# A routing count made by one matrix product, or by two without a clearing, in an attention–MoE–FFN kernel

## The chip, the cores and the metric

The kernel runs on one core of one Trainium2 chip. Its time is the device time of one launch in microseconds; the kernel before was run three times, with a median of 765.33 us (763.8 to 768.46). One further execution was taken by the hardware profiler; every row below is from that one. The core's engines are PE (TensorE, the matrix engine; PEld is its weight load), DVE (VectorE), ACT (ScalarE), POOL (GpSimd) and SP (SyncE, which here only issues transfers). Each engine works through its own list of instructions in order.

## The reference, cut to what matters

Three stages follow each other, all in float32. Four batches of 576 tokens, eight heads of 64, go through an attention with 128 random features; the 2304 tokens of 512 that result go through a mixture of experts (the best of 8 experts by a gate, weighted by its probability); and the result goes through a feed-forward layer of width 2048.

```python
def phi(x):
    h = np.einsum('bhsd,md->bhsm', x, omega) - np.sum(x * x, axis=-1, keepdims=True) / 2.0
    return np.exp(h - np.max(h, axis=-1, keepdims=True)) / np.sqrt(m)
kv = np.einsum('bhsm,bhsd->bhmd', k_p, v)
num = np.einsum('bhsm,bhmd->bhsd', q_p, kv)          # attn = num / (q_p . sum(k_p) + 1e-6)
logits = x @ w_gate                                   # x: attn, (2304, 512); w_gate: (512, 8)
expert_idx = np.argmax(logits, axis=1)
for e in range(E):
    mask = expert_idx == e
    out[mask] = gate_w[mask, None] * (np.maximum(x[mask] @ w1[e], 0.0) @ w2[e])
h = out @ w_in
return (h * (1.0 / (1.0 + np.exp(-1.702 * h)))) @ w_out
```

## The kernel before, in words

**Tiling.** A batch has 576 tokens: four tiles of 128 and a last one with 64 used rows (`T` is 4, `TAIL` is 64). Heads are taken in quads of four, so there are eight quads, `i` = 0 to 7, two to a batch. For each quad, keys and queries are loaded by SP (`m`, L253 and L258), split into two float16 halves (`hl`, ACT L307 and POOL L308), transposed by a transfer from chip memory to chip memory that SP issues (`DMA_TRANSPOSE xT<-hl`, L309), and multiplied with omega on PE (`pr`, L350 and L351). DVE takes maxima (L359, L368) and subtracts (`qp`, `kp`, L380), ACT takes the exponential (L376, L386). Queries are turned on PE (`tq`, L430, with ACT `qpT`, L432) and multiplied with `kv` (`num`, L444); the result is turned back (`tx`, L464; its last 64 rows go to `small`, L466) into the token matrix `xh`/`xl`, two halves whose sum is the float32 value.

**Routing.** When both quads of batch b are done, `route_steps` runs for it: the logits (`lT`, `lg_ps`, `lg`), the row maximum `rm` (L549), the one-hot `oh` (L551, 128 rows by 5 tiles by 8 experts; in tile 4 the rows from 64 on hold no token), the clearing of these rows (L552), the exponentials `ex`, and the count per expert: a product of a matrix of ones with `oh` (`ct_ps`, L561), summed over the tiles (`ct`, L565). The largest count (`cm`, `ci`) gives the batch's main expert `es` (L571). SP reads `es` into a register (L604) and loads that expert's weights, each transfer one `st` (L674). ACT and POOL (for some, DVE) split each into halves `wh` (L698) and `wl` (L700).

**Experts and the rest.** The expert's products on PE (`m_ps`, L136, three products to one of float32) run between the attention steps of the next batches, with `h1h` on ACT (L732) and `h1l` on DVE (L735). The tokens that chose another expert than the batch's main one are counted (`total`); a general path at the end, which is not entered with these inputs, would treat them. From about 400 us on PE does the feed-forward layer (`qa`, L1146 and L1249).

**What sets the order.** The program is written as generators that take turns. Then a scheduler goes over the whole program: it simulates the engines with its own costs, and each engine's list comes out in the order that this simulation gives. One operation that becomes shorter or is gone changes the simulated times, and with them the lists of all engines. Accumulator banks are shared by name: `lT_ps`, `lg_ps`, `ct_ps` and some of the `num` use the one bank "n", so what is written there next waits for the reading of what was there before. In the lists below, [waits ...] names the counters that an instruction waits for; DMAHW0 to DMAHW7 are dealt in turn to the transfers, and the issue of a transfer waits until the earlier one with the same counter has landed.

Of the kernel before, what the change touches and what calls it, by code (L numbers as in the profile page):

```python
# [22 lines left out]
def kernel(  # L23
# [13 lines left out]
    nc = tc.nc  # L37
# [6 lines left out]
    T = 4  # L44
    TAIL = S - T * P
# [97 lines left out]
    ones = const.tile([P, P], F32, name="ones")  # L143
# [367 lines left out]
    def route(b):  # L511
        g = route_steps(b)
        while True:
            with tc.high_priority() if b < HP_ROUTE else nullcontext():
                c = next(g, "end")
            if c == "end":
                return
            yield c

    def route_steps(b):  # L520
# [14 lines left out]
        for t in range(T + 1):  # L535
# [13 lines left out]
        nc.vector.tensor_reduce(out=rm, in_=lg, axis=AX.X, op=ALU.max)  # L549
        oh = att.tile([P, T + 1, E], F32, tag="oh", name="oh", bufs=2)  # L550
        nc.vector.tensor_tensor(out=oh, in0=lg, in1=rm.to_broadcast([P, T + 1, E]), op=ALU.is_equal)  # L551
        nc.vector.memset(oh[TAIL:, T, :], 0.0)  # L552
        ex = att.tile([P, T + 1, E], F32, tag="ex", name="ex", bufs=2)
        nc.vector.tensor_tensor(
            out=ex, in0=lg, in1=rm.to_broadcast([P, T + 1, E]), op=ALU.subtract
# [3 lines left out]
        yield 0  # L559
        ct_ps = pp.tile([P, T + 1, E], F32, tag="n", name="ct_ps", bufs=1)  # L560
        nc.tensor.matmul(  # L561
            out=ct_ps.rearrange("p t e -> p (t e)"), lhsT=ones, rhs=oh.rearrange("p t e -> p (t e)")
        )
        ct = att.tile([P, E], F32, tag="ct", name="ct", bufs=2)
        nc.vector.tensor_reduce(out=ct, in_=ct_ps.rearrange("p t e -> p e t"), axis=AX.X, op=ALU.add)  # L565
        cm = att.tile([P, 8], F32, tag="cm", name="cm", bufs=2)
# [9 lines left out]
        if b == B - 1:  # L576
            dg = att.tile([P, T * P + TAIL], F32, tag="dg", name="dg", bufs=1)
            for t in range(T + 1):
                n = P if t < T else TAIL
                nc.scalar.activation(  # L580
                    out=dg[:n, t * P:t * P + n], in_=ident[:n, :n], func=ACTF.Copy, scale=gate[:n, t, :]
# [5 lines left out]
        for t in range(T + 1):  # L587
# [9 lines left out]
            out=rr[:, :, 0:1], in0=eq, scalar=-float(2 * E), in1=ixf, op0=ALU.mult, op1=ALU.add  # L597
# [12 lines left out]
            out=r_dram[b * S:b * S + T * P].rearrange("(p t) c -> p t c", t=T), in_=rr[:, 0:T]  # L610
# [380 lines left out]
    def general_w(pool, f, s):  # L991
        raw = load_raw(pool, s, f)
        w = pool.tile([P, DM], I32, tag="dec", name="dec", bufs=2)
        decode(w, raw)
        hi = pool.tile([P, DM], F32R, tag=f"w{s}h", name=f"w{s}h", bufs=2)
        lo = pool.tile([P, DM], F32R, tag=f"w{s}l", name=f"w{s}l", bufs=2)
        split(hi, lo, f32(w))
        return hi, lo

    if True:  # L1000
# [399 lines left out]
        p = hp.tile([P, SETW], F32R, tag="y2", name="p2", bufs=1)  # L1400
# [29 lines left out]
    with tc.If(more > 0), tc.tile_pool(name="gp", bufs=1) as gp:  # L1430
        with tc.For_i(0, NT // P, 1) as w:
# [21 lines left out]
            with tc.For_i(0, E, 1) as e:  # L1453
# [6 lines left out]
                with tc.If(cnt > 0):  # L1460
# [3 lines left out]
                    for f in range(NF1):  # L1464
                        wa = gp.tile([P, KD, P], F32, name="wa", bufs=2)
                        nc.sync.dma_start(
                            out=wa,
# [5 lines left out]
                        for kk in range(KD):  # L1473
                            nc.tensor.matmul(
                                out=ps, lhsT=wa[:, kk], rhs=xT[:, kk], start=(kk == 0), stop=(kk == KD - 1)
# [4 lines left out]
                    for dt in range(KD):  # L1480
                        wb = gp.tile([P, NF1, P], F32, name="wb", bufs=2)
                        nc.sync.dma_start(
                            out=wb,
# [5 lines left out]
                        for f in range(NF1):  # L1489
                            nc.tensor.matmul(  # L1490
                                out=ps, lhsT=wb[:, f], rhs=ha[:, f], start=(f == 0), stop=(f == NF1 - 1)
# [6 lines left out]
                    for f in range(NF2):  # L1498
                        wh, wl = general_w(gp, f, 0)
                        oh, ol = general_w(gp, f, 1)  # L1500
# [44 lines left out]
```

## Time and profile before

| what | value |
|---|---|
| median of three runs | 765.33 us (763.8 to 768.46) |
| profiled execution, its time | 766.79 us |
| its span, first to last instruction | 764.9 us |
| instructions | 14360 |
| PE busy | 737.1 us, 96% of the span |
| PEld, DVE busy | 715.1 us (93%), 527.5 us (69%) |
| ACT, POOL busy | 337.5 us (44%), 131.8 us (17%) |

A busy share tells how much of the span an engine had an instruction under way. PE's 27.8 us without one are in a few places; the granted clock (PEclk, in parts of full speed, where 1.00 is 2.4 GHz and 0.50 is 1.2 GHz) tells where a busy PE worked at half its speed. A transfer has two times: how long SP was held by issuing it (the row's own time), and how long it took from the start of the issue to its landing.

### The profile page before, as it was taken

To read this page: it belongs to the slowest core of one execution; us is meant where nothing else is said; L and a number is where in the kernel's file an instruction comes from. 1 tells how busy PE (TensorE), PEld (TensorE's weight loads), DVE (VectorE), ACT (ScalarE), POOL (GpSimd) and SP (SyncE) were. 2 spreads that over 40 slices of the span, in tenths; PEclk is the share of its full clock that TensorE was granted. 3 is DMA by queue.
4 is the path that set the end of the run, shared out by engine and by line. 5 is a ranking of instruction groups with operands and counts; after the bars stand their busy time and mean duration, and the time that the engine had idled before them with its cause. 6 is when DMAs were issued, how large, how long until landed. Compare 5 with 4: busy or idle time off the path is not lost.

```text
span 764.9 us, 14360 instructions
## 1 busy us (share of the span) xinstructions
PE 737.1 (96%) x5559; PEld 715.1 (93%) x5559; DVE 527.5 (69%) x1188; ACT 337.5 (44%) x638; POOL 131.8 (17%) x78
## 2 busy tenths in 40 slices
PE   7998799998999999999999999999999999999997
PEld 6877789998999999998999999999999999999996
DVE  5866848583958577655879559981368777777774
ACT  5554554334623423332427565454576443444331
POOL 3563467604900522000000000000000000000000
PEclk9999799999999999999999999999999999999999
DMA  5447495539723544558155548972978544443311
GB/s 156 116 134 187 160 234 110 136 83 250 189 71 98 169 164 141 175 172 274 59 165 197 178 167 299 320 259 101 330 276 297 171 138 138 138 126 121 114 30 31
DMA packets 136715, 127.57 MB, mean 167 GB/s; under 512 B 58176, under 2 KB 120896, under 8 KB 135744
## 3 DMA queue, kind: packets, MB, share of 16 engines
q1 hardware_dynamic: 123936, 98.85, 44.6%
q10 hardware_dynamic: 12704, 27.73, 10.5%
q8 instruction: 45, 0.74, 0.4%
q14 instruction: 30, 0.25, 0.1%
HBM read 79.68 MB, written 40.40 MB: 157 GB/s over the span
## 4 chain that ended last, share of the span: by engine, by line
PE 80%; DMA 7%; DVE 5%; POOL 3%; ACT 2%; issue 2%; SPq 1%; ACTq 0%; POOLq 0%; DVEq 0%
PE m_ps L136 17%; PE qa L1249 13%; PE qa L1146 13%; PE qm L1249 7%; PE w_ps L136 5%; DMA st<-in_moe_w_dram 4%; PE pb L1249 3%; PE qm L1146 3%; PE qu L1146 3%; PE num L444 2%; POOL wl L700 2%; PE kv_ps L402 2%; PE qn L1146 2%; PE qt L1146 2%; DMA m<-in_k_dram 1%
## 5 line engine op out<-in xcount | busy, mean ns | idle before, releaser
L1146 PE MATMUL qa<-y,wi 128*128 128x384 f32 x576 | 109.2, 337 | 0.4 <-DVE g L901 0.4
L1146 PEld LDWEIGHTS qa<-y,wi 128*128 128x128 f32 x576 | 101.4, 188 | 0.8 <-DVE g L901 0.8
L136 PE MATMUL m_ps<-xh,wh 128*128 128x288 f32 x256 | 77.8, 304 | 0.7 <-DVE h1l L735 0.7
L136 PE MATMUL m_ps<-xh,wl 128*128 128x288 f32 x256 | 76.0, 298 | 0.0
L136 PE MATMUL m_ps<-xl,wh 128*128 128x288 f32 x256 | 75.8, 296 | 0.0
L700 POOL TENSOR_TENSOR wl<-st,wh 128x1024 fp32r<-128x1024 f32 x23 | 55.1, 2403 | 108.2 <-ACT wh L698 108.2
L359 DVE TENSOR_REDUCE small<-pr 128x4 f32<-128x512 f32 (+1 forms) x80 | 51.0, 638 | 16.1 <-PE pr L351 12.3
L698 ACT ACTIVATE wh<-st 128x1024 fp32r<-128x1024 f32 (+1 forms) x33 | 34.0, 1033 | 44.0 <-DMA st<-in_moe_w_dram 32.7
L735 DVE SCALAR_TENSOR_TENSOR h1l<-m_ps,h1h 128x288 fp32r<-128x288 f32 x64 | 28.9, 454 | 34.0 <-ACT h1h L732 34.0
L732 ACT ACTIVATE h1h<-m_ps 128x288 fp32r<-128x288 f32 x64 | 25.8, 405 | 55.3 <-PE m_ps L136 53.9
L136 PEld LDWEIGHTS m_ps<-xh,wh 128*128 128x128 f32 x256 | 48.1, 188 | 1.7 <-DVE h1l L735 1.4
L136 PE MATMUL m_ps<-h1h,wh 128*128 128x288 f32 x160 | 49.2, 307 | 0.0
L136 PEld LDWEIGHTS m_ps<-xl,wh 128*128 128x128 f32 x256 | 48.1, 188 | 0.1
L136 PEld LDWEIGHTS m_ps<-xh,wl 128*128 128x128 f32 x256 | 48.0, 188 | 0.2
L136 PE MATMUL m_ps<-h1h,wl 128*128 128x288 f32 x160 | 47.7, 298 | 0.3 <-POOL wl L700 0.3
L136 PE MATMUL m_ps<-h1l,wh 128*128 128x288 f32 x160 | 47.6, 297 | 0.0
L1249 PE MATMUL qa<-p,p 128*128 128x256 f32 x360 | 46.1, 282 | 1.1 <-DVE p L855 0.8
L1249 PE MATMUL qa<-p,gs 128*128 128x256 f32 x360 | 45.9, 282 | 0.0
L1249 PEld LDWEIGHTS qa<-p,p 128*128 128x128 f32 x360 | 44.1, 189 | 1.6 <-DVE p L855 1.0
L1249 PEld LDWEIGHTS qa<-p,gs 128*128 128x128 f32 x360 | 44.2, 189 | 0.0
L432 ACT ACTIVATE qpT<-tq 128x512 f32<-128x512 f32 (+1 forms) x40 | 22.1, 552 | 43.3 <-PE tq L430 38.6
L444 PE MATMUL num<-kv,qpT 128*128 128x65 f32 (+1 forms) x320 | 39.4, 267 | 0.7 <-ACT qpT L432 0.6
(213 smaller groups left out, 1835.1 us busy)
## 6 DMA issues: line engine op xcount, KB each, us to landing
g_dram<-g ACTq DMA_DIRECT2D x48, 384.0 KB, 3.9
st<-in_moe_w_dram SPq DMA_DIRECT2D x31, 512.0 KB, 5.0
pg<-g_dram SPq DMA_DIRECT2D x10, 1024.0 KB, 5.5
raw<-in_moe_w_in_dram SPq DMA_DIRECT2D x16, 512.0 KB, 3.8
gt<-g_dram SPq DMA_DIRECT2D x8, 1024.0 KB, 5.4
p<-wo_dram SPq DMA_DIRECT2D x6, 1024.0 KB, 7.3
yt<-y_dram SPq DMA_DIRECT2D x12, 384.0 KB, 5.4
vm<-in_v_dram SPq DMA_DIRECT2D x32, 128.0 KB, 3.2
```

The lines of the kernel that those rows point to most:

```text
L136: ins = nc.tensor.matmul(out=ps, lhsT=a, rhs=b, start=start and n == 0, stop=stop and n == 2)
L359: nc.vector.tensor_reduce(out=pm, in_=ps[:, :w], axis=AX.X, op=ALU.max, negate=on_act)
L402: nc.tensor.matmul(out=kv_ps[:, h, :], lhsT=kp[j // 2][:, j % 2, h2, :], rhs=vm[:, h, t, :], start=(t == 0), stop=False,)
L432: nc.scalar.activation(out=qt[i][:, :w], in_=tq[:, :w], func=ACTF.Exp)
L444: nc.tensor.matmul(out=ps[:n, c, h2, :], lhsT=lhsT, rhs=kv[:, h, :])
L698: nc.scalar.activation(out=hi[:, :, s], in_=st[:, :, s], func=ACTF.Copy)
L700: eng.tensor_tensor(out=lo[:, :, s], in0=st[:, :, s], in1=f32(hi)[:, :, s], op=ALU.subtract)
L732: nc.scalar.activation(out=hh[:, f], in_=ps, func=ACTF.Relu)
L735: nc.vector.scalar_tensor_tensor(out=hl[:, f], in0=ps, scalar=0.0, in1=f32(hh[:, f]), op0=ALU.max, op1=ALU.subtract)
L1146: ins = nc.tensor.matmul(out=ps, lhsT=w[:, a, ks], rhs=y[:, b, kk], start=start and kk + m == 0, stop=kk == 1 and m == 2, skip_group_check ...
L1249: ins = nc.tensor.matmul(out=ps, lhsT=x[:, f], rhs=w[i][:, f], start=start and f + m == 0, stop=f == NP - 1 and m == 2, skip_group_check=True,
```

## The change

The clearing L552 goes. The product L561, which took all 128 rows of all five tiles (128x40), becomes one over the four full tiles (128x32) and one over the last tile that takes only its 64 used rows (128x8). Both write the same bank, and what follows reads it as before.

```diff
         nc.vector.tensor_tensor(out=oh, in0=lg, in1=rm.to_broadcast([P, T + 1, E]), op=ALU.is_equal)
-        nc.vector.memset(oh[TAIL:, T, :], 0.0)
         ex = att.tile([P, T + 1, E], F32, tag="ex", name="ex", bufs=2)
...
         ct_ps = pp.tile([P, T + 1, E], F32, tag="n", name="ct_ps", bufs=1)
         nc.tensor.matmul(
-            out=ct_ps.rearrange("p t e -> p (t e)"), lhsT=ones, rhs=oh.rearrange("p t e -> p (t e)")
+            out=ct_ps[:, 0:T].rearrange("p t e -> p (t e)"), lhsT=ones, rhs=oh[:, 0:T].rearrange("p t e -> p (t e)")
         )
+        nc.tensor.matmul(out=ct_ps[:, T], lhsT=ones[:TAIL, :], rhs=oh[:TAIL, T])
         ct = att.tile([P, E], F32, tag="ct", name="ct", bufs=2)
```

The lists of all engines change with it, from the first batch's routing to that of the last (PE up to about 340 us by the trace's times); behind that PE's list is the same. Three places follow.

**DVE, behind the first batch's one-hot.** `ct` is the sum over the tiles, `es` the expert's number that SP waits for; `qp`, `small` and `mx` belong to the attention, `gate`, `ixf`, `eq` and `rr` to the rest of the routing. Before:

```order
L565 TENSOR_REDUCE ct<-ct_ps 128x8
L573 TENSOR_REDUCE gate<-ex 128x5
L368 TENSOR_TENSOR small<-small,sq 128x2
L568 MAX cm<-ct 128x8
L574 TENSOR_SCALAR gate<-gate 128x5
L368 TENSOR_TENSOR mx<-small,sq 128x2
L569 MAX_INDEX ci<-cm,ct 128x8
L575 RECIPROCAL gate<-gate 128x5
L380 TENSOR_TENSOR qp<-pr,mx 128x256
L359 TENSOR_REDUCE small<-pr 128x4
L571 CAST es<-ci 128x1
```

Now:

```order
L565 TENSOR_REDUCE ct<-ct_ps 128x8
L591 CAST ixf<-lix 128x5
L380 TENSOR_TENSOR qp<-pr,mx 128x512
L359 TENSOR_REDUCE small<-pr 128x2
L568 MAX cm<-ct 128x8
L573 TENSOR_REDUCE gate<-ex 128x5
L368 TENSOR_TENSOR small<-small,sq 128x2
L569 MAX_INDEX ci<-cm,ct 128x8
L574 TENSOR_SCALAR gate<-gate 128x5
L368 TENSOR_TENSOR mx<-small,sq 128x2
L571 CAST es<-ci 128x1
```

`ct` now stands ahead of `ixf`, the 128x512 `qp` and a `small` that preceded it before; the 128x256 `qp`, the reciprocal and the 128x4 `small`, which stood ahead of `es`, now stand behind it.

**SP, behind the first eight weight transfers of the first batch.** `r_dram` are routing results, the ISA rows belong to the weight transfer's address, and the transpose brings the halves of one later quad. Before:

```order
L674 DMA st<-in_moe_w_dram 128x2x512 [waits DMAHW0_49]
L609 DMA r_dram<-rr 128x8 [waits DMAHW1_49,DVE_49]
L674 ISA
L674 DMA st<-in_moe_w_dram 128x2x512 [waits DMAHW2_49,DVE_49]
L612 DMA r_dram<-rr 64x2 [waits DMAHW3_49]
L309 DMA_TRANSPOSE xT<-hl 128x18x128 [waits DMAHW4_49,PE_49,Pool_49]
L504 DMA x_dram<-xn 64x256 [waits DMAHW6_49,DVE_49]
```

Now:

```order
L674 DMA st<-in_moe_w_dram 128x2x512 [waits DMAHW0_49]
L609 DMA r_dram<-rr 128x8 [waits DMAHW1_49,DVE_49]
L612 DMA r_dram<-rr 64x2 [waits DMAHW2_49]
L309 DMA_TRANSPOSE xT<-hl 128x18x128 [waits DMAHW3_49,PE_49,Pool_49]
L674 ISA
L674 DMA st<-in_moe_w_dram 128x2x512 [waits DMAHW5_49,DVE_49]
L504 DMA x_dram<-xn 64x256 [waits DMAHW6_49,DVE_49]
```

The transpose now goes ahead of the ninth weight transfer, and waits for the counter that the third of them holds, where it waited for the fourth's.

**PE, where the transposed tile is first read.** `LDWEIGHTS xT [waits DMAHW...]` is the first reading of what the transpose of the SP rows brings. Before, behind a `small` at 99.68 us came 24 products `m_ps` with `wh_1049` (three stand here), and then:

```order
L466 MATMUL small<-ident,xn 128x64 [waits DVE_49]
L136 MATMUL m_ps<-xh,wh_1049 128x288 [waits DVE_49]
L136 MATMUL m_ps<-xl,wh_1049 128x288
L136 MATMUL m_ps<-xh,wl_1050 128x288 [waits Pool_49]
...
L466 MATMUL small<-ident,xn 128x64 [waits DVE_49]
L444 MATMUL num<-kv,qpT 128x65 [waits DVE_49,PE_49]
L444 MATMUL num<-kv,qpT 128x65 x3
L464 MATMUL tx<-ident,xn 128x128 x2
L350 LDWEIGHTS xT [waits DMAHW4_49]
L350 MATMUL pr<-wh_117,xT 128x128 [waits Activation_49]
```

Now:

```order
L466 MATMUL small<-ident,xn 128x64 [waits DVE_49]
L350 LDWEIGHTS xT [waits DMAHW3_49]
L350 MATMUL pr<-wh_117,xT 128x128 [waits Activation_49]
L351 LDWEIGHTS xT
L351 MATMUL pr<-wl_118,xT 128x128
...
L350 MATMUL pr<-wh_117,xT 128x128
L136 MATMUL m_ps<-xh,wh_1049 128x288 [waits DVE_49]
L136 MATMUL m_ps<-xl,wh_1049 128x288
L136 MATMUL m_ps<-xh,wl_1050 128x288 [waits Pool_49]
```

The reading now stands directly behind the `small`, and the 24 products with `wh_1049`, a `num` and two `tx` follow it.

## Rows read from the trace of the kernel before

**Rows 1.** Longest waits of PE, 60 to 400 us: total, times, longest.
```profile
PE ct_ps L561 <- DVE oh L552: 4.1, 1, 4.1
PE tx L464 <- ACT qpT L432: 2.2, 1, 2.2
```

**Rows 2.** The one-hot's instructions: duration ns min/median/max, first and last start us.
```profile
L561 PE MATMUL ct_ps<-oh,ones x8: 198/275/415, 80.3 to 317.8; 128*128 128x40 f32 x8
L551 DVE TENSOR_TENSOR oh<-lg,rm x4: 183/188/1433, 77.9 to 314.2; 128x40 f32<-128x40 f32 x4
L552 DVE MEMSET oh<- x4: 65/65/65, 80.1 to 315.2; 64x8 f32 x4
```

**Rows 3.** Timeline of DVE, 77 to 86 us: start us, us, instruction.
```profile
77.92 1.43 DVE L551 TENSOR_TENSOR oh<-lg,rm 128x40 f32<-128x40 f32 x1
...
83.20 0.38 DVE L380 TENSOR_TENSOR qp<-pr,mx 128x256 f32<-128x256 f32 x1
83.50 0.68 DVE L359 TENSOR_REDUCE small<-pr 128x4 f32<-128x512 f32 x1
84.10 0.14 DVE L571 CAST es<-ci 128x1 int32<-128x1 uint32 x1
```

**Rows 4.** Timeline of POOL at the one-hot.
```profile
76.94 2.36 POOL L308 TENSOR_TENSOR hl<-m,hl 128x1152 f16<-128x1152 f32 x1
```

**Rows 5.** Windows: us, busy time (instructions) of five engines, PEclk, DMA share, GB/s.
```profile
51.00:54.00 3.00, 3.00 (x11) 2.53 (x12) 2.60 (x9) 1.12 (x1) 2.02 (x2) 0.50 0.00 0
78.00:80.00 2.00, 0.00 (x0) 0.00 (x0) 2.00 (x12) 0.52 (x3) 1.92 (x2) 0.50 0.00 0
80.00:88.00 8.00, 7.22 (x47) 6.89 (x48) 7.35 (x41) 2.35 (x7) 2.88 (x2) 0.50 0.23 69
104.00:107.00 3.00, 1.14 (x14) 0.90 (x14) 1.61 (x7) 1.58 (x3) 1.83 (x2) 1.00 1.11 110
178.00:182.00 4.00, 1.82 (x22) 1.57 (x20) 0.46 (x1) 1.54 (x2) 1.18 (x1) 1.00 0.85 158
```

**Rows 6.** Timeline of SP's queue, 84 to 108 us: start us, us of issuing.
```profile
84.97 5.03 SPq L674 DMA_DIRECT2D st<-in_moe_w_dram  x8
...
92.92 6.89 SPq L309 DMA_TRANSPOSE xT<-hl  x1
```

**Rows 7.** Weight tile, 88.95 to 89.95 us: the seventh and eighth transfer.
```profile
L674 SPq DMA_DIRECT2D st<-in_moe_w_dram x2: 529/660/792, 88.5 to 89.2; - x2
...
DMA to landing us min/median/max: 8.6/8.9/9.2
```

**Rows 8.** Weight tile, 166.2 to 167 us: the last load ahead of a later transpose.
```profile
L674 SPq DMA_DIRECT2D st<-in_moe_w_dram x1: 394/394/394, 166.3 to 166.3; - x1
...
DMA to landing us min/median/max: 5.0/5.0/5.0
```

**Rows 9.** Transposed tile, 168 to 169 us: that transpose.
```profile
L309 SPq DMA_TRANSPOSE xT<-hl x1: 2927/2927/2927, 168.3 to 168.3; - x1
...
DMA to landing us min/median/max: 9.7/9.7/9.7
```

**Rows 10.** Line 309, all eleven transposes: from issue to landing.
```profile
DMA to landing us min/median/max: 3.9/4.6/13.7
```

**Rows 11.** Timeline of PE, 93 to 120 us; in brackets idle time before, and releaser.
```profile
99.88 0.40 PE L136 MATMUL m_ps<-xh,wh 128*128 128x288 f32 x1
...
104.38 0.39 PE L464 MATMUL tx<-ident,xn 128*128 128x128 f32 x2
106.64 0.23 PE L350 MATMUL pr<-wh,xT 128*128 128x128 f16 x1 [1.86 <-DMA xT<-hl]
```

**Rows 12.** Timeline of ACT, 164 to 184 us.
```profile
179.69 1.06 ACT L698 ACTIVATE wh<-st 128x1024 fp32r<-128x1024 f32 x1 [4.79 <-DMA st<-in_moe_w_dram]
180.65 0.58 ACT L432 ACTIVATE qpT<-tq 128x512 f32<-128x512 f32 x1
```

**Rows 13.** Line 640: the nearest product with 64 rows.
```profile
L640 PE MATMUL small<-dg,ones x2: 272/296/320, 320.2 to 320.3; 64*128 64x64 f32 x2
```

## The prediction

> **What bounds the kernel now.** I read the waits of PE first, since PE is the engine that is nearly always busy. Between 60 and 400 us, the stretch in which the change moves anything, two waits exceed 2 us [rows 1]: 4.1 us on the one-hot, once, and 2.2 us on the exponential `qpT`, once. The first names the clearing L552 as what PE waited for. The rows of the one-hot show how much there is to win [rows 2]: the clearing is 65 ns long and comes four times, and PE waited for it in one batch of four. In that batch the one-hot itself took 1.43 us instead of 0.19, from 77.92 to 79.35 [rows 3], and it ended just behind a POOL instruction that ran from 76.94 to 79.30 [rows 4]. The clearing at 80.1 is 0.75 us behind the one-hot's end, because other instructions stood between them on DVE. So of the 4.1 us only 0.75 + 0.07 = 0.8 hang on the clearing, and 3.3 on the one-hot.
>
> The windows come next, for the clock [rows 5]. PE had been idle for 4.1 us up to the product at 80.3, so since 76.2 [rows 1, 2]; in 78 to 80 the granted clock was 0.50 (1.2 GHz), and it stayed there over all of 80 to 88, with PE busy for 7.22 of 8 us. Two other gaps, of 1.86 and 2.2 us [rows 11, 1], lie in windows whose clock is 1.00 (2.4 GHz) [rows 5]. Last I read the transfers, because the lists now differ in where they stand: eight weight transfers are issued from 84.97 on [rows 6], the eighth, at 89.2, lands 9.2 us later, at 98.4 [rows 7], and the transpose issued at 92.92 lands 13.7 us later [rows 6, 10], at 106.62. PE waited 1.86 us for it, until 106.64 [rows 11].
>
> **The products and the clearing.** The removed clearing saves 0.065 us of DVE each time. The second product costs one more instruction of two passes. One pass of the 128x40 product took 0.198 us at least and 0.275 in the middle [rows 2]; the nearest one with 64 rows took 0.272 to 0.320 [rows 13], with a 64-wide result. These durations overlap within PE, so 0.1 to 0.4 us is what one more product may cost; I take 0.25. In the first batch it lies beside DVE work, in the other three it lies on PE, which waits for nothing there: 3 x 0.25 = **+0.75 us**.
>
> **The first batch's front.** The product can start at 79.4 instead of 80.3. But `num` now stands directly behind it in the same bank and must wait until DVE has summed `ct` (0.18 us at the front of its list, behind a product of 0.3 to 0.6), which takes up the 0.8 us. DVE is busy 7.35 of the 8 us from 80 to 88 [rows 5], with the same work, and the attention steps of PE wait for it. I take **0** for the time at which PE is through with this work; the bounds are 0.8 us later (the new wait, uncovered) and 0.8 us earlier.
>
> **The expert's number, and the weights.** On DVE the 128x256 `qp` and the 128x4 `small` no longer stand ahead of `es`. They held it from 83.20 to 84.10 [rows 3], so `es` comes 0.9 us earlier, and with it all eight weight transfers: the eighth lands at 98.4 - 0.9 = 97.5. The weights are not waited for much behind that, so this gives nothing by itself.
>
> **The transpose, which is the costly term.** On SP the transpose moves ahead of the ninth weight transfer and waits for the third instead of the fourth. It is issued some 2 us earlier. But it stands behind the same eight weight transfers, and these set when it lands: 106.62 was 8.2 us behind the eighth's landing with the ninth still between, and the nearest other case, at 168.3 + 9.7 = 178.0, landed 6.7 us behind its last load ahead, issued at 166.3 and landed at 171.3 [rows 8, 9]. That case also had a weight transfer issued right behind, as this one now has. So I take 97.5 + 6.7 = 104.2. The bounds are the shortest landing, 3.9 us [rows 10], counted from 97.5 although the issue comes earlier: 101.4, or less; and 106.6, as before.
>
> On PE its reader moves forward by the whole stretch from 99.88 to 104.77 (104.38 + 0.39) [rows 11]: 4.9 us of products that used to cover the transfer. PE now comes to the transpose at about 99.9 plus 0.4 for the front's shift and a later `h1h`, so 100.3, and waits until 104.2: 3.9 us where it waited 1.86. The moved work follows behind. The end of this stretch moves by the landing's shift plus the work now behind it: (104.2 - 106.6) + 4.9 = **+2.5 us**. With a landing at 106.6 it is +4.9, with 101.4 it is -0.3, with one before 100.3 it is -1.5 to -1.9.
>
> **The clock behind it.** PE stands idle for 3.9 us. The 4.1 us gap was followed by a clock of 0.50, the 1.86 and 2.2 us gaps were not [rows 1, 5]; 3.9 is nearest to the first, so I take a fall. Its price is half the time for which a busy PE then works at 0.50: 1.5 us from the 3 us at 51 to 54, in which PE had work all the time as it would have here, 3.6 from the 7.22 at 80 to 88 [rows 5]. Nearest is the stretch with dense work: **+1.5 us**; bounds 0 and 3.6. The Trainium skill's page "TensorE: Matmul & The Clock Gate", section "HAM oscillation — how this bites in real kernels", speaks against this change in the same way: a wait on a transfer between two runs of products makes the next run start at the lower clock, so that the wait costs more than its length. By it the term is in the sum; without it, the sum is 1.5 us less.
>
> **The second batch's wait.** At 179.69 ACT began to split a weight tile for which it had waited 4.79 us, and `qpT` at 180.65 stood behind it, which PE waited 2.2 us for [rows 12, 1]. In the new list of ACT `qpT` stands ahead of that splitting. I take **-2.0 us**; bounds -2.2, and 0 if the transposed queries or keys are late instead.
>
> **The sum** is 0.75 + 0 + 2.5 + 1.5 - 2.0 = +2.75 us on the profiled execution's 766.79 us, 769.5. The median shown, 765.33, is 1.46 us below that execution, and is what a new median will be held against: **768.1 us**. From 400 us on PE's list is the same, so the shift is carried to the end.
>
> **Rivals.**
>
> *The transposed tile is there in time.* If the transpose's small packets run between those of the loads, or start the moment these drain, it lands before PE comes, at 100.3 or sooner. For it: it is issued 2 us earlier, and transposes with an empty queue landed in 3.9 us [rows 10]. Against it: both transposes behind weight loads took 9.7 and 13.7 us. Then the 1.86 us go and the clock stays: 0.75 - 1.9 - 2.0 = -3.1, **762.2 us**. The Trainium skill's "DMA: Bandwidth & Descriptors", section "Latency and other measured facts", gives a transpose 261 GB/s; for 0.59 MB an estimate by that page is 2.3 us, by which it would land about 99.8. No run here shows such a rate behind loads.
>
> *Slower: the transpose does not move at all and the clock pays in full.* The ninth weight transfer, now issued behind it, competes with it as the loads ahead did; it lands at 106.6 as before, PE waits 6.3 us, the clock stays low for as long as at 80 to 88, and the second batch finds another late transfer: 0.75 + 4.9 + 3.6 + 0 = +9.3, **774.6 us**. It decides when the landing comes behind about 105.5 and the low clock lasts over 5 us. For it: all three parts are seen in rows. Against it: they have to come together.
>
> *The front wins.* PE idles 3.3 us instead of 4.1 at 76.2, and the clock might not fall there. At full clock 7.22 us of work would be 3.6 shorter, but DVE's 7.35 busy us in the same 8 leave at most 0.8 of it. With the 0.8 of the wait that is -1.6 against the forecast: **766.5 us**; with the first rival 760.6.
>
> *Nothing is changed that counts.* The clearing is 0.26 us in all, the waits only change their names, the late transpose and the second batch's gain cancel: 765.33 + 0.75 = **766.1 us**.
>
> **How the numbers follow.** Forecast 0.43, transpose in time 0.20, slower 0.12, the front 0.08, nothing 0.17. The bounds of the forecast's own terms, not all at once, give 764 to 772. The range must leave out 0.2: it goes from 761.8, below the first rival, to 772.8, under the slower case, with a tail of each. One per cent, about what a measurement of this kernel can tell from no change, is 7.65 us: faster means below 757.7, slower above 773.0. Only the first two gains together with something unseen reach the one, so 0.03; the slower rival and the forecast's upper tail reach the other, 0.11; within, 0.86.
>
> **What would show it.** In the changed profile: a one-hot product at about 79.4 with a `num` waiting behind it; `es` near 83.2 and the first `st` near 84.0; a transpose issued at 90 to 91 and landed at 104; PE's longest wait at 100 to 104, on the transposed tile, and a PEclk of 0.50 within 102 to 108; no wait on `qpT` near 181. The prediction is wrong if PE does not wait at 100, if the clock stays at 1.00 there, or if a wait of over 1 us stands at a place that I have not named.

## The result, and the profile after

The changed kernel takes **774.98 us** (median of 4 runs, 773.85 to 776.96) beside 766.89 us of the kernel before (4 runs, 763.8 to 771.53): a ratio of **1.0122**, interval 1.0082 to 1.0162. (The ratio is estimated from the runs of both kernels together; it is not the quotient of the two medians, which is 1.0105 here.) It is slower, and outside the range that was predicted. The profiled execution took 775.57 us, its span is 773.8 us.

The waits of PE in the changed kernel, 60 to 420 us (total, times, longest; the five largest):

```profile
PE tx L464 <- DVE xn L455: 3.8, 1, 3.8
PE ct_ps L560 <- DVE ex L553: 2.5, 1, 2.5
PE m_ps L136 <- POOL wl L700: 1.6, 1, 1.6
PE small L466 <- DVE xl L473: 1.3, 1, 1.3
PE tq L430 <- ACT qpT L432: 1.0, 1, 1.0
```

Against [rows 1] the wait for the counting product went from 4.1 to 2.5 us, the one on `qpT` at 181 is gone, and there is none on the transposed tile (compare [rows 11]). The 1.0 us on `qpT` is a new wait, at 94 us in the first batch; it comes back below. At the top stands one that the kernel before did not have: the transposition `tx` waits 3.8 us for the normalised rows `xn`. Its surroundings on PE:

```profile
184.10 1.00 PE L444 MATMUL num<-kv,qpT 128*128 128x65 f32 x8
184.94 0.39 PE L464 MATMUL tx<-ident,xn 128*128 128x128 f32 x2
...
191.34 0.69 PE L464 MATMUL tx<-ident,xn 128*128 128x128 f32 x2 [3.77 <-DVE xn L455]
```

The `num` from which DVE makes `xn` was through at 185.1, yet `xn` comes at 190.86. DVE's timeline in that stretch, with the idle time ahead of a row and its releaser in brackets:

```profile
189.52 0.23 DVE L473 TENSOR_TENSOR xl<-small,xh 128x64 fp32r<-128x64 f32 x1 [7.52 <-ACT xh L469]
...
190.46 0.15 DVE L446 TENSOR_SCALAR rd<-num 128x4 f32<-128x4 f32 x1
...
190.66 0.17 DVE L449 RECIPROCAL rd<-rd 128x4 f32<-128x4 f32 x1
...
190.86 0.42 DVE L455 TENSOR_TENSOR xn<-num,rd 128x256 f32<-128x256 f32 x1
```

DVE stood idle for 7.52 us. At the head of its queue was `xl<-small`, the low halves of 64 routed columns, which needs the high halves `xh` from ACT; `rd` and `xn`, ready for four microseconds, stood behind it. ACT's timeline shows what held `xh`:

```profile
188.32 1.06 ACT L698 ACTIVATE wh<-st 128x1024 fp32r<-128x1024 f32 x1 [3.21 <-DMA st<-in_moe_w_dram]
189.28 0.21 ACT L469 ACTIVATE xh<-small 128x64 fp32r<-128x64 f32 x1
189.38 1.17 ACT L630 ACTIVATE gb<-row 128x512 f32<-128x512 f32 x2
190.44 2.21 ACT L307 ACTIVATE hl<-m 128x1152 f16<-128x1152 f32 x2
192.55 1.05 ACT L698 ACTIVATE wh<-st 128x1024 fp32r<-128x1024 f32 x1
193.50 0.40 ACT L732 ACTIVATE h1h<-m_ps 128x288 fp32r<-128x288 f32 x1
193.79 0.60 ACT L469 ACTIVATE xh<-tx 128x512 fp32r<-128x512 f32 x1
```

It is the splitting of a weight tile, `wh`, which waited 3.21 us for its transfer. So a transfer that PE does not need yet holds ACT, ACT holds DVE, and DVE holds PE: the lists of two engines, each worked through in order, pass the wait on. The same stretch of DVE in the kernel before:

```profile
187.27 0.16 DVE L446 TENSOR_SCALAR rd<-num 128x4 f32<-128x4 f32 x1 [0.70 <-PE num L444]
187.47 0.18 DVE L449 RECIPROCAL rd<-rd 128x4 f32<-128x4 f32 x1
187.68 0.42 DVE L455 TENSOR_TENSOR xn<-num,rd 128x256 f32<-128x256 f32 x1
...
191.02 0.23 DVE L473 TENSOR_TENSOR xl<-small,xh 128x64 fp32r<-128x64 f32 x1 [2.00 <-ACT xh L469]
```

There `xl<-small` was even later, at 191.02, and cost PE nothing, because `rd` and `xn` stood ahead of it. Then the clock. Windows of the changed kernel (columns as in [rows 5]):

```profile
175.00:189.00 14.00, 12.56 (x109) 11.89 (x108) 2.82 (x10) 4.01 (x7) 4.79 (x2) 1.00 0.99 262
189.00:203.00 14.00, 11.66 (x64) 11.60 (x65) 7.86 (x24) 7.95 (x13) 13.55 (x7) 0.52 0.65 169
```

and the second of them in the kernel before:

```profile
189.00:203.00 14.00, 13.73 (x132) 13.33 (x131) 11.39 (x33) 11.07 (x18) 13.14 (x6) 1.00 0.80 227
```

In the same 14 us PE carried out 64 products instead of 132, at a granted clock of 0.52, nearly all of it the lower level (1.2 GHz), where the kernel before had 1.00 (2.4 GHz). The first 2.3 us of these 14 belong to the wait.

**Where 8.9 us went in this execution.** Two losses of PE were worked out for each stretch from windows of 1 us: the idle time, and the clock's share (busy time x (1 - PEclk)). FFN start is PE's first product of L1146. "Again" is the changed kernel profiled a second time; the last two columns are experiments below (e11 and e12).

| stretch, us | before: idle + clock | changed | again | both places | before, both places |
|---|---|---|---|---|---|
| 0 to 70 | 8.0 + 1.7 | 9.3 + 0 | 7.6 + 3.3 | 8.6 + 0 | 8.1 + 0 |
| 70 to 100 | 6.2 + 3.7 | 5.8 + 4.1 | 8.1 + 4.2 | 6.0 + 3.2 | 6.2 + 2.7 |
| 100 to 175 | 2.2 + 0 | 1.6 + 0 | 2.4 + 1.7 | 0.5 + 0 | 0.7 + 0 |
| **175 to 215** | **2.4 + 0** | **3.8 + 5.9** | 1.8 + 0 | 3.8 + 0 | 2.1 + 0 |
| 215 to 420 | 2.0 + 0 | 1.7 + 1.7 | 1.4 + 0 | 1.0 + 0 | 1.7 + 0 |
| sum | 20.8 + 5.4 | 22.1 + 11.7 | 21.3 + 9.2 | 19.8 + 3.2 | 18.9 + 2.7 |
| FFN start | 399.78 | 408.66 | 405.05 | 398.48 | 395.41 |

Of the 8.88 us by which the changed kernel comes later to the FFN, 1.3 are idle time, 6.3 the clock, and the remaining 1.3 are work. The stretch 175 to 215 alone has 7.3.

Each column is one execution, and that limits what the table can tell. Up to 175 us the changed kernel, its repeat and the version with both places mended have the same order of instructions on PE and DVE, yet their idle and clock losses there come to 20.8, 27.3 and 18.3 us. Such differences are not the doing of any edit. In the repeat the stretch 175 to 215 lost 1.8 us, less than the 2.4 of the kernel before, and the kernel was slow all the same. So the 7.3 us explain the first profiled execution; that the place costs time in the median has to come from the experiments.

### The profile page after: what moved, and what is told of

Read it like the earlier page. It is cut to its first block, busy times and chain, and to the rows that moved or that the text cites. A ratio compares the mean times of both kernels' runs of the same rounds, so it can differ in the third digit from the quotient of the medians.

```text
span 773.8 us, 14380 instructions
## 1 busy us (share of the span) xinstructions
PE 744.6 (96%) x5567; PEld 722.2 (93%) x5567; DVE 526.0 (68%) x1184; ACT 338.2 (44%) x638; POOL 132.0 (17%) x78
## 4 chain that ended last, share of the span: by engine, by line
PE 83%; DMA 6%; DVE 4%; issue 2%; POOL 2%; ACT 2%; SPq 1%; ACTq 0%; POOLq 0%; DVEq 0%
PE m_ps L136 18%; PE qa L1249 13%; PE qa L1146 13%; PE qm L1249 7%; PE w_ps L136 5%; PE pb L1249 3%; PE qm L1146 3%; PE qu L1146 3%; PE num L444 3%; PE kv_ps L402 3%; DMA st<-in_moe_w_dram 2%; DMA m<-in_k_dram 2%; PE pr L344 2%; PE qn L1146 2%; PE tq L430 2%
## 5 line engine op out<-in xcount | busy, mean ns | idle before, releaser
L1146 PE MATMUL qa<-y,wi 128*128 128x384 f32 x576 | 109.2, 337 | 0.4 <-DVE g L901 0.4
L1146 PEld LDWEIGHTS qa<-y,wi 128*128 128x128 f32 x576 | 101.4, 188 | 0.8 <-DVE g L901 0.8
L432 ACT ACTIVATE qpT<-tq 128x512 f32<-128x512 f32 (+1 forms) x40 | 22.1, 554 | 45.9 <-PE tq L430 39.7
```

Of the source, the lines that this page charges most:

```text
L432: nc.scalar.activation(out=qt[i][:, :w], in_=tq[:, :w], func=ACTF.Exp)
L1146: ins = nc.tensor.matmul(out=ps, lhsT=w[:, a, ks], rhs=y[:, b, kk], start=start and kk + m == 0, stop=kk == 1 and m == 2, skip_group_check ...
```

## The experiments

**Theory A**: the cost is queue order in the second batch's stretch, DVE's place (`rd`, `xn` behind `xl<-small`) and then ACT's (`xh<-tx` behind transfers), with the clock as its sequel. Rivals: the second product, or the missing clearing, costs by itself; or the clock falls by chance and the queues only happen to stand near. `follow` below sets the order of two instructions on an engine and adds no wait. Behind such a place the lists are written anew as well: up to about 190 us e1, e10 and e11 have the lists of the changed kernel, behind it PE's order differs up to 241 us in e1 and 264 us in e10 and e11. Each ratio is estimated against runs of the kernel before on the same chip.

**DVE's place mended** (e1). The change, with `xl<-small` of the fifth quad forced behind the quad's last `xn`:

```diff
-                    nc.vector.tensor_tensor(
+                    follow(nc.vector.tensor_tensor(
...
-                    )
+                    ), xn_last[0] if (qi, pr) == (4, 1) and o else None)
```

> The changed kernel with one instruction moved: the subtraction xl<-small of the fifth quad's second half goes behind that quad's last xn on DVE (an order without a wait of its own); everything up to 192 us is otherwise the same on all engines. Theory A (the loss is a queue on DVE: rd and xn stood behind xl, which waited for ACT, which waited behind a weight splitting for a transfer; PE then idled 3.8 us at 187.6 and its clock was 0.50 from 189.5 to 203): no PE wait over 1 us from 180 to 195, clock 1.00 from 175 to 215, time 774.98 - 3.8 - 6 = 765, 763 to 767.5. Rival B (the second product and the new wait of num in the shared bank cost it, in every batch): still 773 to 777. Rival C (the moved transpose of the first batch, as predicted): still 773 to 777.

Measured 767.94 us, **1.0035** (1.0007 to 1.0063; the quotient of the medians is 1.0057). That is 0.4 us above theory A's range. The wait on `xn` is gone; the next place on the same way shows up instead, with a low clock from 196 to 199 us:

```profile
PE tq L430 <- DVE xl L473: 3.5, 1, 3.5
```

The 3.5 us are at 196: ACT's `xh<-tx` stands behind two conversions and a `wh`, as in the fence of ACT above, and `tq` needs that bank.

**ACT's place alone, and the changed kernel again** (e10, e9). The high halves `xh<-tx` go ahead of the conversion and the `wh` that wait for transfers; DVE stays as changed:

```diff
-            nc.scalar.activation(out=hl[:, c, 0], ...)
+            follow(nc.scalar.activation(out=hl[:, c, 0], ...), xh_last.get((4, 1, 0)) if src is k_in and i == 7 else None)
...
-                nc.scalar.activation(out=hi[:, :, s], ...)
+                follow(nc.scalar.activation(out=hi[:, :, s], ...), xh_last.get((4, 1, 0)) if (b, c) == (1, 5) else None)
```

> The changed kernel as it is, timed beside the next three. Theory A (in the second batch the rows of the quad's second half stand behind its transfer on ScalarE and VectorE, and the clock falls after that wait): ratio 1.009 to 1.015, a wait of 3 to 4 us on VectorE near 191 us and half clock behind it. Rival (the first measurement caught slow executions, the change is worth nothing): 1.000 to 1.006.

> The change with one place mended on ScalarE only: the copy of the fifth quad's first half of the transposed rows goes ahead of the two operations that wait for a transfer; VectorE's list stays as changed. Theory A, the VectorE place alone makes the first wait: a wait of 2 to 4 us of TensorE near 188 to 191 us stays, half clock behind it stays, ratio 1.006 to 1.011. Rival, the ScalarE place is what matters and VectorE's order only follows: no such wait, 0.998 to 1.003.

The change again: 772.23 us, **1.0111** (1.0072 to 1.0149). The size repeats, the picture only in part. PE again waits for `xn`, but 1.8 us and not 3 to 4, and no half clock follows it:

```profile
PE tq L430 <- ACT qpT L432: 2.4, 1, 2.4
...
PE tx L464 <- DVE xn L455: 1.8, 1, 1.8
```

In this execution the clock fell elsewhere, as its windows show:

```profile
47.00:55.00 8.00, 7.31 (x26) 6.09 (x27) 5.83 (x18) 3.45 (x9) 6.56 (x4) 0.57 0.14 32
...
95.00:99.00 4.00, 2.89 (x17) 2.83 (x18) 3.40 (x12) 3.68 (x11) 4.00 (x2) 0.57 1.26 199
122.00:126.00 4.00, 3.20 (x17) 3.05 (x18) 1.77 (x6) 0.00 (x0) 4.00 (x3) 0.61 0.10 37
```

With ACT's place mended alone: 771.19 us, **1.0083** (1.0055 to 1.0112). The wait on `xn` stays with 2.1 us and the half clock stands behind it:

```profile
189.00:203.00 14.00, 12.06 (x73) 11.99 (x74) 8.38 (x25) 7.65 (x12) 12.21 (x6) 0.63 0.75 197
```

So DVE's place is the first of the two, as theory A has it; the wait and the half clock that it names for the repeat were wrong, though the ratio lay in its range. e10 also speaks against the new order behind 193 us as the cause of e1's gain: it has such an order too and stays slow.

**Both places** (e11, again as e15; e5, again as e16; e12). Both edits in the change; the same with one more conversion moved from 142 to 190 us, which also changes the order of some loads (`src is q_in and i == 6` in place of `k_in`, 7); and both edits in the kernel before.

> The changed kernel with two places of the lists put right: on DVE as in the first run, and on ACT xh<-tx of the fifth quad's second half ahead of two hl and of a weight splitting that stood ahead of it. Theory A (what was lost lies in these two queues, 3.8 us of idling and 5.9 of low clock in the profile of the changed kernel, 3.5 and 1.6 with the first place alone put right): no PE wait over 1 us from 180 to 200 and clock 1.00 there, ratio to before 0.996 to 1.002. Rival D (the loss is spread over small waits at all routings and the low clock is chance): ratio 1.004 to 1.008, as with the first place alone.

> The change with both places mended, on VectorE (rd, recip and xn ahead of the second half's xl) and on ScalarE, and nothing else moved before 186 us. Theory A: no wait of TensorE over 1 us between 180 and 200 us, idle and clock loss of 175 to 215 us together under 3 us against 9.7 in the changed kernel, ratio 0.997 to 1.003. Rival (two products and the missing clearing cost by themselves, the queues only show it): 1.006 to 1.012.

> The kernel before with the same two places set as in the run ahead, one product and the clearing kept. Theory A: these places were good enough in the kernel before, so 0.996 to 1.001, and the difference to the run ahead, which is the change without its queue order, is within 0.003. Rival (the places are worth time in any kernel, and the change itself costs): 0.990 to 0.995, with the run ahead 0.005 or more above it.

> The change with both places mended, which gave 1.0056, again beside the next. Theory A with a remainder: 1.002 to 1.006. If the two versions are the same within what a measurement tells: both within 0.002 of each other.

> The change with both places mended and one conversion (hl) of the next quad's rows moved from 142 to 190 us, which gave 1.0002, again. If moving the conversion is worth time by itself: 0.998 to 1.002, 0.003 or more under the run ahead. If not: within 0.002 of it.

| kernel | us | ratio | interval |
|---|---|---|---|
| change, both places (e11) | 766.29 | 1.0056 | 1.0030 to 1.0083 |
| the same again (e15) | 766.38 | 1.0033 | 1.0010 to 1.0055 |
| and the conversion moved (e5) | 764.10 | 1.0002 | 0.9979 to 1.0025 |
| the same again (e16) | 764.23 | 1.0013 | 0.9992 to 1.0034 |
| before, both places (e12) | 764.51 | 1.0017 | 0.9990 to 1.0044 |

All four measurements of mended versions lie below the change (the interval of e11 reaches that of the change), and both places are worth nothing to the kernel before. For e11 theory A was off: it is above the 0.997 to 1.003, idle and clock lost 3.8 us from 175 to 215 where under 3 were expected, and two waits stand where none over 1 us was expected, 1.3 us at 191 and 2.5 us at 198, with a full clock behind both (the other 1.5 us on `qpT` are at 93):

```profile
PE tq L430 <- ACT qpT L432: 4.0, 2, 2.5
...
PE tq L430 <- DVE xl L473: 1.3, 1, 1.3
```

Against e12 a remainder of 0.0016 (e15) to 0.0039 (e11) is left, 1.2 to 3.0 us; theory A allowed 0.003. By the table above it is 0.9 idle, 0.5 clock and 1.7 work for e11 (3.07 us at the FFN's start). The moved conversion seems to give 0.002 to 0.005 more, but the intervals overlap: not settled.

**Parts of the change** (e2, e14, e3, e4, e8). Two products with the clearing kept (e2), the same with both places mended (e14), no clearing and one product over all rows, which then counts the last tile's uncleared rows too (e3), and the change in the second batch only (e4) or in the first only (e8):

to the change (e2, e14)

```diff
+        nc.vector.memset(oh[TAIL:, T, :], 0.0)
```

to the kernel before (e3)

```diff
-        nc.vector.memset(oh[TAIL:, T, :], 0.0)
```

to the kernel before (e4; in e8 `(0,)`)

```diff
-        nc.vector.memset(oh[TAIL:, T, :], 0.0)
+        if b not in (1,):
+            nc.vector.memset(oh[TAIL:, T, :], 0.0)
...
+        if b in (1,):
+            nc.tensor.matmul(out=ct_ps[:, 0:T]..., rhs=oh[:, 0:T]...)
+            nc.tensor.matmul(out=ct_ps[:, T], lhsT=ones[:TAIL, :], rhs=oh[:TAIL, T])
...
```

> Only the half of the change that makes two products; the clearing stays, read by nobody. Its DVE list has rd and xn ahead of xl<-small at the place in question, the ACT list has xh<-small behind the weight splitting as in the changed kernel. Theory A: no PE wait over 1 us from 180 to 195, clock 1.00 there, 763 to 768. Rival B (two products cost it): 772 to 777. Rival C (the first batch's new order, which this one shares in part): 770 to 777.

> Two products with the clearing kept, both places mended. Theory A: the second product costs 1 to 2 us in the four batches and the queue the rest, so 1.000 to 1.004, down from 1.0087 without the two places. Rival (the products cost by the clock, which falls at another place when this one is mended): 1.005 to 1.010.

> Only the other half: the clearing goes, the product stays one; the 64 rows without a token then add 64 to every expert's count, which leaves the largest the same. Its DVE list has rd and xn of the last num behind xl<-small as in the changed kernel; on ACT xh<-small stands ahead of that weight splitting, but behind hl, which waits for the keys' load. Theory A: a PE wait of 2 to 4 us near 188 and a low clock behind it, 769 to 776. Rival B (products): 763 to 767, as before. Rival C (first batch): 763 to 777, not told apart here.

> The change in the second batch's routing alone; the first, third and fourth are as before. The lists are those of before up to 150 us; behind it DVE has rd and xn ahead of xl<-small, and ACT has xh<-small ahead of the weight splitting. Theory A: no such wait, 762 to 767, the 2.2 us wait on qpT at 181 gone. Rival B: a quarter of the loss, 767 to 769. Rival C (first batch): 764 to 767.

> The change in the first batch's routing alone. Its lists at 180 to 200 us are those of the kernel that only dropped the clearing, where PE waited under 1 us there. Theory A: no PE wait over 1.5 us there, ratio 0.998 to 1.006, with what is lost elsewhere. Rival C (the first batch's own order, the moved transpose, costs it): 1.008 to 1.015, with a wait on the transposed tile near 100 us.

| kernel | us | ratio | interval |
|---|---|---|---|
| two products, clearing kept (e2) | 770.33 | 1.0087 | 1.0061 to 1.0113 |
| the same, both places (e14) | 765.55 | 1.0020 | 0.9993 to 1.0047 |
| no clearing, one product (e3) | 770.76 | 1.0077 | 1.0049 to 1.0105 |
| the change in the second batch only (e4) | 763.56 | 0.9994 | 0.9966 to 1.0023 |
| in the first batch only (e8) | 765.84 | 1.0021 | 0.9991 to 1.0051 |

e2 has DVE's place right and is slow all the same, which theory A did not expect (763 to 768 us). Its waits show ACT's place at 194, with a low clock from 192 to 198, and a wait on `qpT` at 93, in the first batch:

```profile
PE tq L430 <- DVE xl L473: 2.4, 1, 2.4
PE tq L430 <- ACT qpT L432: 2.3, 1, 2.3
```

With both places mended the same two products are 0.2% slower than the kernel before (interval up to 0.5%). e3, with less work than the kernel before, is as slow as e2. Its time lies in theory A's range, but the wait near 188 us that this range was for did not come (0.9 us at most). The longest new wait of its trace is in the fourth batch, at 353 us: ACT's `h1h` stands behind a `wh` whose transfer is late. That this is what makes e3 slow is argued from one trace, not shown. Its waits:

```profile
PE w_ps L136 <- ACT h1h L731: 3.3, 1, 3.3
```

So neither the second product nor the missing clearing is needed for a loss of this size: e3 has no second product, and e2 keeps the clearing. Each edit writes all queues anew from its first batch on, and part of what is measured is the price of that order.

**DVE's place made bad in the kernel before** (e13). The 64 columns of the second half are transposed and split ahead of `rd` (the new `tail_first` is left out here):

```diff
+            lead = tail_first() if (qi, i) == (4, 3) else None
...
-            nc.vector.tensor_scalar(
+            follow(nc.vector.tensor_scalar(
...
-            )
+            ), lead)
```

> The kernel before, one product and clearing kept, with VectorE's place in the second batch made as in the changed kernel: rd, recip and xn of the fifth quad behind the second half's xl, with the rows around them on ScalarE and TensorE moved with it, and nothing else moved before 182 us. Theory A (the place costs the time, in any kernel): a wait of TensorE on xn of 1 to 4 us near 188 us and perhaps half clock behind it, ratio 1.003 to 1.010. Rival (the place is harmless without the change, whose cost is its products and the clock): 0.997 to 1.002.

Measured 765.09 us, **1.0015** (0.9985 to 1.0045): the rival's range, and PE waits 0.9 us:

```profile
PE tx L474 <- DVE xn L456: 0.9, 1, 0.9
```

So the place does not cost 1% wherever it stands. But e13 is not the changed kernel's place alone. Two things differ in its trace. PE has 29 products `m_ps` between that `num` and the `tx` that waits, where the changed kernel has 17: it is ready for `tx` 5.4 us after the start of `num` (181.81, 187.20), and 3.5 us after it in the changed kernel (184.10, 187.57) and in its repeat (189.82, 193.29). Twelve products take 1.6 us there, so without them the wait would be about 2.5 us, an estimate. And from the start of `num` to that of the `wh` in front of `xh` are 2.5 us here (181.81, 184.28), 4.2 in the changed kernel (184.10, 188.32). The second is not what decides by itself: in the repeat it was 2.2 us (189.82, 192.04), and PE waited 1.8 us.

**PE's gap filled** (e6, e7). Twelve extra 128x40 products ahead of the first batch's count, in the changed kernel and in the one before (written here as a loop):

```diff
+        for _ in range(12 if b == 0 else 0):
+            nc.tensor.matmul(out=ct_ps..., lhsT=ones, rhs=ones[:, 0:40])
```

> The changed kernel with twelve extra 128x40 products on the matrix of ones ahead of the first batch's count, into the same bank, overwritten by the count: they keep PE busy while the one-hot is late, and they add 3 to 4 us of PE work in a gap. Its lists happen to have the order of before at 180 to 200 us: rd and xn ahead of xl<-small, xh<-tx ahead of the second hl. Theory A: no PE wait over 1.5 us from 180 to 200, clock 1.00 there; and if idling is what lowers the clock, it is 1.00 from 76 to 88 too. Ratio 0.990 to 1.001. Rival B (the two products cost it): 1.008 to 1.015.

> The kernel before, its one product and its clearing kept, with the same twelve products ahead of the count. Its lists happen to have the bad order: xl<-small ahead of recip and xn on DVE, and xh<-small behind a weight splitting and hl on ACT. Theory A: a PE wait of 2 to 4 us near 188, a clock of 0.50 behind it for 3 to 14 us, although the routing is the old one; the clock from 76 to 88 stays 1.00, which gives 1 to 3.7 us back; ratio 1.000 to 1.010. Rival B: 0.995 to 1.000 and no wait near 188.

The change so filled: 767.78 us, **1.0050** (1.0029 to 1.0071); the kernel before: 768.99 us, **1.0075** (1.0043 to 1.0107). The first is no slower than the second, though it holds the whole change. e6 lies above theory A's 0.990 to 1.001. PE idled only 1.0 us ahead of the count in it, and the clock was low all the same, 0.67 in this window:

```profile
78.00:85.00 7.00, 5.16 (x40) 4.51 (x37) 6.60 (x29) 1.74 (x5) 1.92 (x2) 0.67 0.17 50
```

In e7 the wait on `qpT` is as long as in the kernel before, 2.2 us, and this time a fall follows:

```profile
180.00:187.00 7.00, 7.00 (x36) 6.70 (x35) 1.50 (x5) 2.60 (x4) 3.89 (x2) 0.51 1.02 340
```

A wait near 188 us, which theory A expected in e7, did not come. So e7 lies in theory A's range for another reason. Filling did not hold the clock, and the length of one wait alone does not tell whether it falls.

**The clock over all runs.** The mean granted clock is known of every run, not only of the profiled one. A run's span x (1 - that clock) is an estimate of what the low clock took; it is too high where the clock was low while PE waited. Means over the runs, in us, less those of the kernel before on the same chip:

| kernel | span | clock's share | rest |
|---|---|---|---|
| changed again (e9) | +8.1 | +4.3 | +3.9 |
| ACT's place mended (e10) | +6.9 | +3.7 | +3.1 |
| DVE's place mended (e1) | +4.2 | +0.7 | +3.4 |
| both places (e11) | +3.8 | -0.6 | +4.3 |
| the same again (e15) | +2.2 | -1.6 | +3.8 |
| two products, clearing kept, both places (e14) | +1.8 | -2.8 | +4.6 |

By this about half of the change's loss is the clock (the six runs of e9 spread from 4.6 to 14.6 us, so no closer), and that half is what goes when DVE's place is mended. The other half, 3 to 5 us of waits and work, stays whichever place of the table is mended (with the conversion moved as well, 0.6 in e5 and 2.5 in e16), and in e11, e14 and e15 a clock better than beside it hides part of it. So the 0.2% of e14 are not the price of its products.

## Why the prediction was wrong

- **The products, right within what can be told.** Taken +0.75 us; the table of the profiled executions leaves 1.3 (changed), 1.0 (again) and 1.7 us (e11 against e12) for all work that is neither idle time nor clock.
- **The first batch's front, beyond its bounds.** The count came at 78.38 (79.4 expected) and `num` waits 0.39 us behind it for `ct`, so far right in kind. The weight transfers start at 82.72 and not at 84.0: 2.25 us earlier, where 0.9 were read from the order. But ACT's list had turned here too. Where `qpT` followed one splitting of 128x1024 before, it now follows three. Before, then changed:

```profile
91.41 1.06 ACT L698 ACTIVATE wh<-st 128x1024 fp32r<-128x1024 f32 x1 [2.17 <-DMA st<-in_moe_w_dram]
92.37 0.58 ACT L432 ACTIVATE qpT<-tq 128x512 f32<-128x512 f32 x1
```

```profile
89.02 1.06 ACT L698 ACTIVATE wh<-st 128x1024 fp32r<-128x1024 f32 x1 [0.80 <-DMA st<-in_moe_w_dram]
90.51 1.06 ACT L698 ACTIVATE wh<-st 128x1024 fp32r<-128x1024 f32 x1 [0.43 <-DMA st<-in_moe_w_dram]
92.01 1.06 ACT L698 ACTIVATE wh<-st 128x1024 fp32r<-128x1024 f32 x1 [0.44 <-DMA st<-in_moe_w_dram]
...
93.57 0.59 ACT L432 ACTIVATE qpT<-tq 128x512 f32<-128x512 f32 x1
```

PE waits for it 1.0 us here and 2.4 in the repeat; "0", with 0.8 us either way, had no room for that. All eleven profiled executions with two products and no filling in the first batch have this wait (1.0 to 2.4 us, at 93 to 96), the other seven do not, and in five of the eleven some 3 us of low clock follow it. It is a candidate for what stays with both places mended; no run mends it, so that is not shown.
- **The transposed tile, wrong, and its rival right.** It was to land at 104.2 and hold PE for 3.9 us. SP's queue in the changed kernel:

```profile
82.72 4.86 SPq L674 DMA_DIRECT2D st<-in_moe_w_dram  x8
...
89.31 6.83 SPq L309 DMA_TRANSPOSE xT<-hl  x1
```

and that transpose's landing:

```profile
DMA to landing us min/median/max: 10.7/10.7/10.7
```

It was there at 100.0, and PE's `pr` began at 100.06 without a wait (its weight load waited 0.2 us): just in time. What failed is the assumption that the tile lands 6.7 us behind the last load ahead: that load, issued at 87.1, took at most 8.9 us, so it landed by 96.0, and the tile 4.0 us behind it or more. The terms +2.5 and +1.5 did not come; by the rival it was -1.9. The Trainium skill's "DMA: Bandwidth & Descriptors", section "Latency and other measured facts", led to an estimate of 99.8 in that rival. The landing agrees with it, but its 0.59 MB in 10.7 us from the issue, behind loads, do not show that page's rate.
- **The second batch's wait, the step that failed.** "I take -2.0 us; bounds -2.2, and 0". The wait on `qpT` did go. But PE only came to the next late transfer sooner: it stood ready for `tx` at 187.57 where it had begun that at 189.95 before, while the `wh` in front started at 188.32 instead of 188.73. With `rd` and `xn` now behind `xl<-small` the 2.2 us were handed back as 3.8, and the clock's 5.9 came on top: in this execution the stretch gave +7.3 where -2.0 was taken, in the repeat -0.6, with a wait of 1.8 us and no fall. The bounds allowed no loss. That the place costs time in the median, and not in one execution only, is what e1 shows against the change (767.94 us and 1.0035, where the change has 1.0111 and 1.0122). I had read the rows of ACT up to 184 us and of DVE's list only the first batch; that DVE's order had turned here was to be read in its list, and that ACT's `xh` hung on a transfer, in the trace of before.
- **The clock.** The fall was forecast at 100 with a price of 1.5 us. In the first profiled execution it came at 189 instead, and cost four times as much; in the repeat there were falls at 95 and 122. Not all of it is the change's doing: up to 70 us, where the change moves nothing, the clock's share is 0 to 3.3 us in the table's columns. The Trainium skill's "TensorE: Matmul & The Clock Gate", section "HAM oscillation — how this bites in real kernels", says that a wait on a transfer makes the products behind it start slowly; 3.8 us in the change and 2.1 in e10 show it (waits that a transfer passed on through ACT or DVE), 1.8 us in the repeat and 2.5 in e11 do not.
- **The rivals.** "Slower" gave 774.6 us, near what was measured, by luck as to the way: two of its parts came, a late transfer in the second batch and a long low clock, but its place, the transposed tile at 106.6, was wrong. Its 0.12 was too little: it asked for three parts together, and the time came about without the first.

**Shown**: mending DVE's place takes the wait on `xn` away and half to two thirds of the loss (1.0122 and 1.0111 to 1.0035; by the quotients of the medians 1.0105 and 1.0114 to 1.0057); with both places 1.0002 to 1.0056 are left; neither the second product nor the missing clearing is needed for a loss of 0.8%. **Argued**: that the queues cost it by the way of the fences, since only the first profiled execution and, with a smaller wait, that of e10 show the whole of it, and since e1 and e11 also write anew what stands behind the places. **Open**: what the 3 to 5 us of waits and work are that stay with both places mended, and what the second product costs in them; why the moved conversion helps, if it does; and whether the bad place costs as much in the kernel before, because e13 also moved twelve products and the transfers' order.

## What to carry to other kernels

Where an edit lets an order be written anew, follow the wait that is said to go away one step further: which late transfer does the engine come to next, and what stands behind the instruction that waits for it, on each queue in between? A removed wait on a busy engine is a gain only if that next transfer comes sooner too; otherwise its bound has to include a loss, with the clock's share. One trace of each kernel does not settle such a story: profile the same kernel twice, and see what differs where the lists are the same. Before a difference of one per cent is put down to the operation that was edited, make the same edit with the queues' order held.

## What had not been expected of the hardware

- A transpose behind eight weight loads occupied SP's queue for 6.83 us while it was issued, and a second one, at 97.54, for 6.34; the loads queued behind it on SP start only then. Where one was issued at 175.51 it took 3.96 us.
- The granted clock fell behind a wait of 2.2 us in one execution (e7) and not in another (before), with the same instruction waiting; and with PE idle for only 1.0 us, behind twelve narrow 128x40 products, it was low all the same (e6).
- Two executions of the same changed kernel lost 5.9 and 0 us to the clock between 175 and 215 and 4.1 and 9.2 us ahead of that; at the FFN's start they differ by 3.6 us.
